# Where the next slot's halves are compared, when q and k are split, and when the ends are turned, in a top-k attention kernel with a feed-forward layer

## The chip, the cores and the metric

The kernel runs on one core of one Trainium2 chip. The metric is the device time of one execution in microseconds (us). Engines are named as in the profile: PE (TensorE; PEld is its weight load), DVE (VectorE), ACT (ScalarE), POOL (GpSimd) and SP (SyncE, which here issues nearly all DMAs).

## The reference

```python
# q, k, v: (8, 8, 576, 64), float32; top_k = 32
scores = (1.0 / np.sqrt(D)) * np.matmul(q, k.transpose(0, 1, 3, 2))
kth = np.partition(scores, -top_k, axis=-1)[..., -top_k:-top_k + 1]
scores = np.where(scores >= kth, scores, -1000000000.0)
scores = scores - np.max(scores, axis=-1, keepdims=True)
attn = np.exp(scores)
attn = attn / (np.sum(attn, axis=-1, keepdims=True) + 1e-09)
x = np.matmul(attn, v).transpose(0, 2, 1, 3).reshape(4608, 512)
h = x @ w_in                                  # (512, 2048)
g = h * (1.0 / (1.0 + np.exp(-1.702 * h)))
out = g @ w_out                               # (2048, 512)
```

Each row of 576 scores keeps its 32 largest; the rest vanish in the softmax. The result goes, head beside head, through a feed-forward layer with a quick GELU.

## The kernel before

**Slots.** The attention is cut into 144 slots, 18 for each batch. A slot is 128 query rows of two heads: four row tiles by four pairs of heads, and two slots that gather the 64 rows left at the end of each head (the "ends"). The first 13 slots (0 to 12, function `slot`) also load and round the weights; from slot 13 on, `two_slots(n)` with odd n lays out two slots at a time. The order of instructions is written out by hand: each engine works off its own queue in the order in which the Python code issues to it, and waits for other engines only through data.

**One slot's way.** `scores` (PE, L295) multiplies q by k into two PSUM tiles. `copy_scores` (ACT, L307) copies them scaled to `sc`. The search (`find`, `topk_of_pairs`, DVE) finds the 32nd largest: `pair_up` compares the halves of each row (L336) into `greater`, and POOL computes the smaller ones without loss in integers, first `sc` less `greater` (L339), then plus the other half (L349) into `lesser`. DVE takes the 32 largest of `greater` by four rounds of MAX8 (L366) with MATCH_REPLACE8 (L369) between them, the 16 largest of `lesser` by two rounds, merges both (L373) and takes the bound, `cut` (L378). `mask` (ACT, L423) and `exps` (ACT, L431, with the sums `den`) follow; `invert` (DVE, L439 and L441) makes the reciprocal `rden`; `normalize` (POOL, L454, two instructions) multiplies. `split` (ACT, L490) parts the words in 16-bit halves over `sc`, SP writes them to DRAM (L492) and reads them back transposed (L498). `values_at` (PE, L557) multiplies by v, and `x_of` (ACT, L571 or L574) copies the result into a row block.

**The feed-forward layer.** Whenever a row block is ready, `hidden` (PE, L618) does a piece of the first layer, for two row blocks together or for one; `tanh` (ACT, L640 and L643) and `gate` (POOL, L652 and L653) make the GELU, and `project` (PE, L673) adds a piece of the second. A finished block leaves through ACT (L681) and SP (L683). One `hidden` and one `project` stand in each slot from slot 13 on, where there is work for them.

**q and k.** They are needed with the head's 64 elements across partitions. `load_both` fetches them (L184, L187) at the slots that `FETCH` gives, counted from a batch's first slot, one entry for each pair of heads. For batch 1, `prepare_by_pe` turns them on PE: `prepare_main` (L217, copied by ACT at L218) and then `prepare_ends` (L222, copied at L223 and L225), which `two_slots` calls through the list `second_part`. From batch 2 on `prepare_by_dma` does it at the slots of `READY`: ACT splits the words into halves (L246), SP writes them to DRAM (L250, L254, L255) and reads them back transposed (L259).

**Within a search.** `find(m)` runs 23 operations: 14 on `greater` (numbers 0 to 13), `pair_up(m + 1)` (14), six on `lesser` (15 to 20), the merge (21) and the bound (22). After number 20 in odd slots and 18 in even ones it calls `invert(m - 1)`. In `two_slots(n)`, POOL's queue gets L339 in the search, then `normalize(n - 1)`, and then `measure(n)`: the lower bounds `lows` (L399), the add of `pair_rest` (L349) and the gate.

Of the kernel before, what the change touches and what calls it, by code (L numbers as in the profile page):

```python
# [9 lines left out]
ALU = mybir.AluOpType  # L10
ENG = mybir.EngineType
F32 = mybir.dt.float32
U32 = mybir.dt.uint32
I32 = mybir.dt.int32
# [4 lines left out]
P = 128  # L19
# [11 lines left out]
def kernel(  # L31
# [27 lines left out]
    nc = tc.nc  # L59

    B, H, S, D = q.shape
# [6 lines left out]
    HALF = S // 2  # L68
# [23 lines left out]
    raws = pool("raws", 7)  # L92
# [24 lines left out]
    raw = {}  # L117
# [154 lines left out]
    second_part = []  # L272
# [8 lines left out]
    N = len(slots)  # L281
    PER = N // B
    st = [{} for _ in slots]
# [45 lines left out]
    greater, lesser = {}, {}  # L329

    def pair_up(n):

        sc = st[n]["sc"]
        a, b = sc[:, :, 0:HALF], sc[:, :, HALF:S]
        greater[n] = lefts.tile([P, 2, HALF], F32, name="greater", tag="left")
        nc.vector.tensor_tensor(out=greater[n][:], in0=a, in1=b, op=ALU.max)  # L336
        lesser[n] = raws.tile([P, 2, HALF], F32, name="lesser", tag="raw")
        whole = lesser[n][:].bitcast(I32)
        nc.gpsimd.tensor_tensor(out=whole, in0=a.bitcast(I32), in1=greater[n][:].bitcast(I32), op=ALU.subtract)  # L339
        unpaired.append(n)  # L340

    unpaired = []
# [1 line left out]
    def pair_rest():  # L344

        while unpaired:
            n = unpaired.pop()
            whole, b = lesser[n][:].bitcast(I32), st[n]["sc"][:, :, HALF:S]
            nc.gpsimd.tensor_tensor(out=whole, in0=whole, in1=b.bitcast(I32), op=ALU.add)  # L349

    def topk_of_pairs(n):

        top = st[n]["top"] = small.tile([P, 2, 2 * TOPK], F32, name="top2", tag="top")
        cut = st[n]["cut"] = small.tile([P, 2], F32, name="cut")
        first, few = greater.pop(n), lesser.pop(n)
        left = lefts.tile([P, 2, HALF], F32, name="left2", tag="left")

        def found(r, i, written=False):
            if r < TOPK // 8:
                at = (8 * r + TOPK) % (TOPK + TOPK // 2)  # L360
                return top[:, i, at : at + 8]
            end = 2 * TOPK - 8 * (r - TOPK // 8) - TOPK
            return top[:, i, end - 1 : end - 9 : -1] if written else top[:, i, end - 8 : end]

        def largest(src, r, i):
            nc.vector.max(found(r, i, True), src[:, i, :])  # L366

        def remove(to, src, r, i):
            nc.vector.match_replace(to[:, i, :], found(r, i), src[:, i, :], LOWEST)  # L369

        def merge():
            both = top[:, :, 0:TOPK].rearrange("p i (s k) -> p i k s", s=2)
            nc.vector.tensor_reduce(  # L373
                out=top[:, :, TOPK + TOPK // 2 :], in_=both, axis=mybir.AxisListType.X, op=ALU.max
            )

        def bound():
            nc.vector.tensor_reduce(  # L378
                out=cut[:], in_=top[:, :, TOPK + TOPK // 2 - 1 :], axis=mybir.AxisListType.X, op=ALU.min, negate=True
            )  # L380

        ops = []
        for r in range(TOPK // 8):
            ops += [lambda r=r, i=i: largest(left if r else first, r, i) for i in range(2)]
            if r < TOPK // 8 - 1:
                ops += [lambda r=r, i=i: remove(left, left if r else first, r, i) for i in range(2)]
        ops += [lambda: pair_up(n + 1) if n + 1 < N else None]
        for r in range(TOPK // 8, TOPK * 3 // 16):
            ops += [lambda r=r, i=i: largest(few, r, i) for i in range(2)]
            if r == TOPK // 8:  # L390
                ops += [lambda r=r, i=i: remove(few, few, r, i) for i in range(2)]
        return ops + [merge, bound]

    def lows(n):

# [40 lines left out]
    def invert(n):  # L436

        some = small.tile([P, 2], F32, name="some", tag="sums")
        nc.vector.tensor_scalar_add(some[:], st[n]["den"][:], 1e-9)  # L439
        rden = st[n]["rden"] = small.tile([P, 2], F32, name="rden", tag="inverse")  # L440
        nc.vector.reciprocal(rden[:], some[:])  # L441
# [44 lines left out]
    def split(n):  # L486

        pr, sc = st[n]["pr"], st[n]["sc"]
        halves = sc[:].rearrange("p i k -> p (i k)").bitcast(U16).rearrange("p (h k) -> p h k", h=2)
        nc.scalar.copy(out=halves, in_=pr[:].bitcast(U16).rearrange("p (k h) -> p h k", h=2))  # L490
        rows = st[n]["rows"] = apart.tile([P, 2, 2 * S], U16, name="rows")
        nc.sync.dma_start(rows[:], halves)  # L492
# [209 lines left out]
    def at(n, fn, *args):  # L702
        later.setdefault(n, []).append((fn, args))
# [1 line left out]

    READY = (-13, -11, -5, -3)
    READY_1 = (-5, -3, -1, 1)
    FETCH = (-17, -15, -9, -7)  # L710
    FETCH_1 = (-11, -9, -4, -2)
    VALUES = (0, 1, 2, 3)
    by_slot = dict(enumerate([2, 2, 3, 3, 3, 3, 3, 3, 3, 3, 2, 2]))
# [12 lines left out]
    for b in range(1, B):  # L726
        for hp in range(NP):
            at(b * PER + (FETCH if b > 1 else FETCH_1)[hp], load_both, b, hp)
            if b > 1:
                at(b * PER + READY[hp], prepare_by_dma, b, hp)  # L730
            else:
# [6 lines left out]
    def finish_one():  # L738
        unfinished.pop(0)()

    def may_project(waiting):

        return len(to_project) > waiting and len(finished) >= NG * CC + to_project[0][1][-1] + 1
# [62 lines left out]
    def bring_all():  # L806

        waiting = len(ready)
        while put_off:
            put_off.pop(0)()  # L810
        if len(ready) > waiting:
            hidden()
# [90 lines left out]
    def two_slots(n):  # L903

        preparing = prepare_by_dma, prepare_by_pe
        todo = [later.pop(m, []) for m in (n, n + 1)]
        live = lambda m: 0 <= m < N
        aside = n < N
        opens = n == SETTLED + 1
        ahead = n < SETTLED + 4  # L910
        assert not any(fn in preparing for fn, _ in todo[1])

        def begin(some):
            for fn, args in some:
                if fn not in preparing:
                    fn(*args)

        def prepare_some():
            for fn, args in todo[0]:
                if fn in preparing:  # L920
                    fn(*args)

        def find(m):
            for i, op in enumerate(topk_of_pairs(m) if live(m) else [lambda: None] * 23):
                op()
                if i == (20 if m % 2 else 18) and live(m - 1):
                    invert(m - 1)
                if i > 1 and unfinished:
                    finish_one()

        def measure(m):
            if live(m):
                lows(m)
            pair_rest()
            gate(aside)

        def project_one():
            if may_project(0):
                project(True)

        if opens:
            bounds(n - 1)
            gate(aside)
        if ahead:
            scores(n + 2)
        if opens:
            bring_all()
        if live(n - 1):
            exponentials(n - 1)
        if ahead:  # L950
            copy_scores(n + 2)
        if opens:
            leave_all()
            tanh(aside)
        prepare_some()
        hidden(ps_t if opens else None)
        while second_part:
            second_part.pop()()
        project_one()
        find(n)  # L960
        if live(n - 1):
            normalize(n - 1)
        tanh(aside)
        measure(n)
        if live(n - 1):
            split(n - 1)
        begin(todo[0])
        if live(n):
            mask(n)
        held = [m for m in (n - 3, n - 2) if live(m) and "rows" in st[m]]  # L970
        if live(n + 2) and not ahead:
            scores(n + 2)
            copy_scores(n + 2)
        o = ps_t.tile([P, 2, P], F32, name="o", tag="tp") if held else None
        for i, m in enumerate(held):
            values_at(m, o[:, i, :])
        if live(n - 1):
            turn_by_dma(n - 1)
        while turns:
            turns.pop(0)()  # L980
        if live(n + 3):
            scores(n + 3)
        if live(n):
            exps(n)
        if held:
            x_of(held, o)
        leave_all()
        hidden(ps_t)
        if live(n + 3):
            copy_scores(n + 3)  # L990
        find(n + 1)
        if live(n):
            normalize(n)
            split(n)
        begin(todo[1])
        if live(n):
            turn_by_dma(n)
        tanh(aside)
        measure(n + 1)
        project_one()  # L1000
        leave_all()
# [39 lines left out]
```

## Time and profile before

| | |
|---|---|
| median of 3 runs | 1469.41 us (1468.19 to 1469.87) |
| the profiled execution's own time | 1469.86 us |
| its span | 1468.0 us |
| busy: PE, PEld, DVE, ACT, POOL | 97%, 69%, 91%, 79%, 66% |
| mean granted clock of TensorE | 0.987 |
| DMA queues, share of 16 engines' span | 62.8% (the main one) |

The profile is one execution. Its span runs from the first instruction to the last; the execution's own time is 1.9 us longer. A busy share is an average over stages: the first 240 us, in which weights are rounded and batch 1 is prepared, the long middle to about 1390 us, in which pairs of slots repeat, and the end, in which the last row blocks go through the feed-forward layer. In the profile each matmul of the source is two instructions. Rows of a group give its source line, engine, operation, output and input tiles, shapes and count; a wait gives the engine and tile that waited, what released it, total us, times and the longest.

### The profile page before, as it was taken

To read this page: it belongs to the slowest core of one execution; us is meant where nothing else is said; L and a number is where in the kernel's file an instruction comes from. 1 tells how busy PE (TensorE), PEld (TensorE's weight loads), DVE (VectorE), ACT (ScalarE), POOL (GpSimd) and SP (SyncE) were. 2 spreads that over 40 slices of the span, in tenths; PEclk is the share of its full clock that TensorE was granted. 3 is DMA by queue.
4 is the path that set the end of the run, shared out by engine and by line. 5 is a ranking of instruction groups with operands and counts; after the bars stand their busy time and mean duration, and the time that the engine had idled before them with its cause. 6 is when DMAs were issued, how large, how long until landed. Compare 5 with 4: busy or idle time off the path is not lost. (4 is left out here: it accounts for less than half of the span.)

```text
span 1468.0 us, 29154 instructions
## 1 busy us (share of the span) xinstructions
PE 1428.0 (97%) x9564; PEld 1006.4 (69%) x9564; DVE 1337.2 (91%) x4672; ACT 1154.8 (79%) x1865; POOL 970.8 (66%) x1171
## 2 busy tenths in 40 slices
PE   7789989999999999999999999999999999999998
PEld 5667746777666667777666667777666667777665
DVE  7999999999999999999999999999999999999910
ACT  6998787878788887878888787888878787778730
POOL 3777666676676776666767667667677666677610
PEclk8899999999999999999999999999999999999999
DMA  7452266767677676776678676776768776644530
GB/s 220 142 156 73 64 169 172 203 170 190 160 196 191 181 176 181 199 183 171 173 189 191 180 180 169 203 185 173 186 175 189 179 192 169 165 131 130 136 88 15
DMA packets 516312, 242.04 MB, mean 165 GB/s; under 512 B 452672, under 2 KB 490560, under 8 KB 516160
## 3 DMA queue, kind: packets, MB, share of 16 engines
q1 hardware_dynamic: 515728, 239.89, 62.8%
q8 instruction: 75, 1.23, 0.4%
q14 instruction: 77, 0.63, 0.1%
q10 hardware_dynamic: 432, 0.30, 0.1%
HBM read 45.09 MB, written 102.24 MB: 100 GB/s over the span
## 5 line engine op out<-in xcount | busy, mean ns | idle before, releaser
L618 PEld LDWEIGHTS ph<-xT,win 128*128 128x128 f32 x3520 | 484.7, 191 | 89.0 <-issue 52.6
L618 PE MATMUL ph<-xT,win 128*128 128x128 f32 (+1 forms) x3520 | 538.0, 309 | 3.8 <-ACT xT L574 2.9
L673 PE MATMUL po<-wout,th 128*128 128x512 f32 x1152 | 522.3, 596 | 0.0
L490 ACT COPY sc<-pr 128x2304 uint16<-128x2304 uint16 x132 | 279.0, 2113 | 153.8 <-POOL pr L454 153.7
L673 PEld LDWEIGHTS po<-wout,th 128*128 128x128 f32 x1152 | 214.8, 192 | 214.5 <-issue 209.0
L366 DVE MAX8 top<-left 128x8 f32<-128x288 f32 x792 | 320.9, 446 | 0.0
L339 POOL TENSOR_TENSOR lesser<-sc,greater 128x576 int32<-128x576 int32 x132 | 186.3, 1411 | 195.2 <-DVE greater L336 194.5
L454 POOL TENSOR_SCALAR pr<-pr,rden 128x576 f32<-128x576 f32 x264 | 194.1, 748 | 125.8 <-DVE top L373 85.9
L369 DVE MATCH_REPLACE8 left<-top,left 128x288 f32<-128x288 f32 x528 | 229.6, 442 | 0.0
L431 ACT ACTIVATE pr<-sc,low 128x576 f32<-128x576 f32 x288 | 219.6, 767 | 0.0
L366 DVE MAX8 top<-lesser 128x8 f32<-128x288 f32 x528 | 213.7, 446 | 0.0
L423 ACT ACTIVATE sc<-sc,cut 128x576 f32<-128x576 f32 x288 | 207.4, 770 | 6.5 <-POOL cut L410 3.8
L295 PE MATMUL s_ps<-qk_t 64*128 64x288 f32 (+1 forms) x1280 | 190.3, 433 | 0.2 <-ACT qk_t L218 0.2
L349 POOL TENSOR_TENSOR lesser<-lesser,sc 128x576 int32<-128x576 int32 x132 | 186.5, 1413 | 0.2
L307 ACT ACTIVATE sc<-s_ps 128x576 f32<-128x576 f32 x288 | 170.3, 644 | 4.8 <-PE s_ps L295 3.4
L653 POOL TENSOR_TENSOR th<-th,h 128x512 f32<-128x512 f32 x129 | 165.3, 1282 | 10.8
L295 PEld LDWEIGHTS s_ps<-qk_t 64*128 64x128 f32 (+1 forms) x1280 | 106.2, 178 | 80.1 <-issue 57.8
L640 ACT ACTIVATE th<-ph 128x512 f32<-128x512 f32 x144 | 85.5, 594 | 76.0 <-PE ph L618 72.1
L557 PE MATMUL o<-pt,v_l 128*64 128x128 f32 (+1 forms) x2368 | 143.5, 264 | 0.0
L557 PEld LDWEIGHTS o<-pt,v_l 128*64 128x64 f32 x2368 | 119.8, 137 | 26.9 <-issue 18.4
L336 DVE TENSOR_TENSOR greater<-sc 128x576 f32<-128x576 f32 x132 | 99.8, 756 | 40.0 <-ACT sc L307 40.0
L652 POOL TENSOR_SCALAR th<-th 128x512 f32<-128x512 f32 x129 | 80.0, 620 | 57.7 <-ACT th L640 57.7
(78 smaller groups left out, 1386.6 us busy)
## 6 DMA issues: line engine op xcount, KB each, us to landing
rows<-sc SPq DMA_DIRECT2D x132, 576.0 KB, 3.2
qk_rows<-halves SPq DMA_DIRECT2D x48, 256.0 KB, 2.8
qk_l<-in_q_dram SPq DMA_DIRECT2D x64, 128.0 KB, 3.3
raw<-in_moe_w_in_dram SPq DMA_DIRECT2D x16, 512.0 KB, 4.6
v_l<-in_v_dram SPq DMA_DIRECT2D x32, 256.0 KB, 3.7
raw<-in_moe_w_out_dram SPq DMA_DIRECT2D x16, 512.0 KB, 3.5
out_dram<-ob SPq DMA_DIRECT2D x32, 256.0 KB, 2.9
qk_l<-in_k_dram SPq DMA_DIRECT2D x62, 128.0 KB, 3.0
```

What stands on the lines that cost most here:

```text
L295: nc.tensor.matmul(ps[i][rows, c, 0:HALF], lhsT=qT[b, hps[p]][on, cols], rhs=kT[b, hps[p]][on, FIRST[i] + c * HALF : FIRST[i] + (c + 1) * ...
L339: nc.gpsimd.tensor_tensor(out=whole, in0=a.bitcast(I32), in1=greater[n][:].bitcast(I32), op=ALU.subtract)
L349: nc.gpsimd.tensor_tensor(out=whole, in0=whole, in1=b.bitcast(I32), op=ALU.add)
L366: nc.vector.max(found(r, i, True), src[:, i, :])
L369: nc.vector.match_replace(to[:, i, :], found(r, i), src[:, i, :], LOWEST)
L423: nc.scalar.activation(sc[:, i, :], sc[:, i, :], AF.Prelu, bias=cut[:, i : i + 1], alpha=HUGE)
L431: nc.scalar.activation(pr[:, i * S : (i + 1) * S], sc[:, i, :], AF.Exp, bias=low[:, i : i + 1], accum_out=den[:, i : i + 1],)
L454: nc.gpsimd.tensor_scalar(pr[:, i, :], pr[:, i, :], st[n]["rden"][:, i : i + 1], 1.0, op0=ALU.mult, op1=ALU.mult)
L490: nc.scalar.copy(out=halves, in_=pr[:].bitcast(U16).rearrange("p (k h) -> p h k", h=2))
L557: nc.tensor.matmul(o[j * D : (j + 1) * D, cols], lhsT=main[:, j, c, :] if c < NF else tail[:, j, :], rhs=pt[:, MAIN[j] + c if c < NF else ...
L618: nc.tensor.matmul(ph[:, i * many * P : (i + 1) * many * P], lhsT=win[:, c, f * P : (f + 1) * P], rhs=xs[:, first : first + step * (many - ...
L673: nc.tensor.matmul(x.po[:], lhsT=gT[:, i * P : (i + 1) * P], rhs=wout[:, f, :], start=(x.done == 0), stop=(x.done == FC - 1))
```

## The change

Three things move.

- The next slot's halves are compared after the bound of a search, as its last operation, and no longer between the rounds on `greater` and those on `lesser`. POOL's subtract moves from there into `pair_rest`, directly ahead of the add. The numbers of the operations on `lesser` fall by one, and the reciprocal of the sums is called after number 17 in odd slots (after the removals from `lesser`) and 19 in even ones (after its second maxima).
- The slots at which q and k are split for batches 2 to 7 change from -13, -11, -5, -3 to -13, -9, -5, -1, counted from the batch's first slot, and the third fetch from -9 to -11.
- The ends of batch 1's q and k (slots 13, 15, 17 and 19) are turned behind the projection, the search's issue and the split of the slot before, and no longer ahead of the projection.

```diff
@@ pair_up
         nc.vector.tensor_tensor(out=greater[n][:], in0=a, in1=b, op=ALU.max)
-        lesser[n] = raws.tile([P, 2, HALF], F32, name="lesser", tag="raw")
-        whole = lesser[n][:].bitcast(I32)
-        nc.gpsimd.tensor_tensor(out=whole, in0=a.bitcast(I32), in1=greater[n][:].bitcast(I32), op=ALU.subtract)
         unpaired.append(n)
@@ pair_rest
             n = unpaired.pop()
-            whole, b = lesser[n][:].bitcast(I32), st[n]["sc"][:, :, HALF:S]
+            a, b = st[n]["sc"][:, :, 0:HALF], st[n]["sc"][:, :, HALF:S]
+            lesser[n] = raws.tile([P, 2, HALF], F32, name="lesser", tag="raw")
+            whole = lesser[n][:].bitcast(I32)
+            nc.gpsimd.tensor_tensor(out=whole, in0=a.bitcast(I32), in1=greater[n][:].bitcast(I32), op=ALU.subtract)
             nc.gpsimd.tensor_tensor(out=whole, in0=whole, in1=b.bitcast(I32), op=ALU.add)
@@ topk_of_pairs
-        ops += [lambda: pair_up(n + 1) if n + 1 < N else None]
         for r in range(TOPK // 8, TOPK * 3 // 16):
...
-        return ops + [merge, bound]
+        return ops + [merge, bound, lambda: pair_up(n + 1) if n + 1 < N else None]
@@ the schedule
-    READY = (-13, -11, -5, -3)
+    READY = (-13, -9, -5, -1)
...
-    FETCH = (-17, -15, -9, -7)
+    FETCH = (-17, -15, -11, -7)
@@ find
-                if i == (20 if m % 2 else 18) and live(m - 1):
+                if i == (17 if m % 2 else 19) and live(m - 1):
                     invert(m - 1)
@@ two_slots
         hidden(ps_t if opens else None)
-        while second_part:
-            second_part.pop()()
         project_one()
         find(n)
...
             split(n - 1)
+        while second_part:
+            second_part.pop()()
         begin(todo[0])
```

## The prediction

> **What bounds the kernel now.** I read the page first, then the busy time by stage, the waits, and the timelines of PE, ACT, DVE and POOL over one repeat of the work. The page's busy lines say that PE is full and DVE close behind:
>
> ```profile
> PE 1428.0 (97%) x9564; PEld 1006.4 (69%) x9564; DVE 1337.2 (91%) x4672; ACT 1154.8 (79%) x1865; POOL 970.8 (66%) x1171
> ```
>
> By stage, in a stretch of the middle (columns: stretch, length, busy PE, PEld, DVE, ACT, POOL, clock, DMA share, GB/s):
>
> ```profile
> 440.00:640.00 200.00, 200.00 (x1296) 140.24 (x1295) 191.29 (x698) 163.90 (x253) 139.42 (x169) 1.00 0.72 186
> ```
>
> PE never pauses there, and DVE idles 8.7 us of 200. A busy PE can still be a stretched one, so I took the time from the first scores of one pair of slots to those of the next, in PE's timeline. Quiet pairs take 18.65 us while the first layer's matmuls serve two row blocks (719.71 to 738.36), 18.89 while they serve one (586.16 to 605.05), and inside them each matmul follows the last at its shortest spacing (0.215 us for 256 columns). DVE, read from one cut (L378) to the same a pair later, has its own rate: 18.79 us in quiet pairs of either sort. Two loops of almost the same length run side by side, and two sorts of stall sit on top. The waits name the first:
>
> ```profile
> DVE greater L336 <- ACT sc L307: 40.0, 63, 1.3
> ```
>
> Once in a pair DVE stands still, 0.5 us in quiet pairs, because the next slot's scores are not yet copied. With the overlap of successive instructions that is lost there (0.08) it is 0.6, so DVE's own work is about 18.2 us a pair; the pair 185.96 to 204.12, in which it never waits, took 18.16. The second stall shows in ACT's timeline:
>
> ```profile
> 617.03 0.60 ACT L681 ACTIVATE ob<-po 128x512 f32<-128x512 f32 x1 [1.40 <-PE po L673]
> ...
> 620.37 2.10 ACT L246 COPY halves<-qk_l 128x2304 uint16<-128x2304 uint16 x1
> ...
> 623.33 2.12 ACT L490 COPY sc<-pr 128x2304 uint16<-128x2304 uint16 x1
> ...
> 626.69 1.18 ACT L307 ACTIVATE sc<-s_ps 128x576 f32<-128x576 f32 x2
> ```
>
> An output block leaves (L681, behind a wait of 1.40 for PE), and a preparation of q and k (L246, 2.1 us) follows in the same pair. ACT is late for L307, and the scores that need those PSUM tiles are stretched on PE from 1.24 to 1.72:
>
> ```profile
> 608.54 1.24 PE L295 MATMUL s_ps<-qk_t 64*128 64x288 f32 x8
> ...
> 627.43 1.72 PE L295 MATMUL s_ps<-qk_t 64*128 64x288 f32 x8
> ```
>
> **What the Trainium skill says.** "Perfetto Trace Analysis", Identifying the Most-Contended Engine, holds that matmul busy time does not tell how full TensorE is; here 100% busy goes with both 18.65 and 19.73 us a pair, hence the spacings above. The same page, Optimization Strategy, says that a gap repeated on the engine that should be full can mean too little PSUM: so here, the two score tiles not being emptied in time. "SBUF — State Buffer", Who interferes with whom, says that a DVE instruction with two SBUF inputs and a GpSimd instruction that reads SBUF exclude each other, whole instructions long, the first to start winning. The trace has it once:
>
> ```profile
> 153.11 1.29 POOL L144 TENSOR_TENSOR wout<-wout,raw 128x512 int32<-128x512 int32 x1
> 153.28 1.73 DVE L336 TENSOR_TENSOR greater<-sc 128x576 f32<-128x576 f32 x1
> 154.47 1.69 POOL L147 TENSOR_TENSOR wout<-wout,raw 128x512 f32<-128x512 f32 x1
> ```
>
> The comparison, 0.74 us elsewhere, ended 0.61 after POOL's instruction; POOL's next, 1.29 elsewhere, took 1.69. All other 131 comparisons now start while POOL is idle or in its last 0.1 us.
>
> **The change, part by part.** No instruction is added or removed; their order moves.
>
> (1) The spacing. Preparations move in each batch from slots -13, -11, -5, -3 to -13, -9, -5, -1. In the trace L681 falls in slots 25, 29, 33, 39, 43, 47, 51, 55, 57, 61, 65, 69 and so on. Every second preparation of two (25, 33, 43, 51, 61, 69) meets one, no first one does (23, 31, 41, 49, 59, 67), and the new places (27, 35, 45, 53, 63, 71) are free of it. Stalled pairs on PE, less the quiet 18.65 or 18.89 (and 0.17 where an end slot's values take 2.49 instead of 2.32): 0.48, 0.91, 0.59, 0.43, that is 2.4 us in each 36 slots, three times over batches 2 to 7: 7.2 us. A lone preparation (599.59) costs PE nothing and I cost the new places at nothing; what hides it is ACT's wait for POOL (0.84 there) ahead of L490. Loads move with it: six DMA issues at -11 instead of -9. They hold SP some 5 us (589.47 to 594.15 at another slot) ahead of a transpose of probabilities; the values that need it start at 606, after its landing at about 599. The buffer it fills is free since -13. The last k and q (slot -1) land some 5 us after issue, 7 us ahead of their scores. Cost 0.
>
> (2) The comparison at the end of the search. The scores are there 3 us earlier than needed, so the 0.6 us goes. Late next would be the inverse of the sums (L439), which waits for exps (L431): in slots with an L681 these end (620.47) just as the inverse is reached today, so DVE will wait there up to 1.5 us in every second pair. PE does not feel it while DVE has slack. On POOL the subtract (1.41) now stands behind the two multiplies and lows, directly ahead of the add; POOL's idle time ahead of it (194.5 us in all) covers it. The add is done some 5.7 us after the reciprocal at worst, and its result is read at some 7.5 (the comparison and 14 operations later); the gate behind it feeds a projection 3.2 us after its end (712.98 to 716.18) and starts at most 1.4 later. Cost 0.
>
> But the comparison now falls beside POOL's multiplies, which start 0.33 after the reciprocal and read SBUF:
>
> ```profile
> 716.33 0.17 DVE L441 RECIPROCAL rden<-some 128x2 f32<-128x2 f32 x1
> 716.42 0.20 DVE L373 TENSOR_REDUCE top<-top 128x32 f32<-128x64 f32 x1
> 716.65 0.19 DVE L378 TENSOR_REDUCE cut<-top 128x2 f32<-128x34 f32 x1
> 716.66 0.75 POOL L454 TENSOR_SCALAR pr<-pr,rden 128x576 f32<-128x576 f32 x1 [1.25 <-DVE top L373]
> 716.75 0.81 DVE L366 MAX8 top<-greater 128x8 f32<-128x288 f32 x2
> ```
>
> With R for the reciprocal's start, POOL multiplies from R+0.33 to 1.07 and 1.07 to 1.80. In odd slots a pair of MAX8 comes between, and the comparison starts at R+1.28, inside the second: by the instance above it ends at 1.80+0.61 = 2.41 instead of 2.02, 0.4 late. In even slots it starts where the last line shows, R+0.42, 0.09 after POOL. If POOL holds the port it ends at 1.07+0.61 = 1.68 instead of 1.16, 0.5 late; if DVE does, POOL loses 0.6, which is hidden. POOL's start is not its first read: L147 above was held until 0.54 after its start and lost 0.39, so it needs the port about 0.15 in, and a multiply by a pointer sets up longer (0.27 for one element at L399, 0.19 for two at L411). I take DVE as first, by little. So DVE needs 18.2+0.4 = 18.6, or 19.1.
>
> (3) The ends behind the projection, four times (slots 13 to 19). PE's waits there (3.2 and 3.9 longest) vanish, but two of the four lie where PE has no first-layer work and DVE sets the pace. ACT's copies of the ends now follow a projection of 3.6 us, which can delay mask by 0.8 in slots 13 and 15. Between -1.6 (DVE's waits up to there: 1.08 and 0.52) and +1; I take 0.
>
> **Sum.** With DVE at 18.6, PE sets the pace: 7.2 from (1), and 0.4 in each 36 slots (over slots 20 to 142, 1.4) that PE now loses to DVE's 18.79 when it runs at 18.65, of which I take half. 1469.86 - 7.9 = 1462.0 against the profiled execution's own time; the median of the runs lies 0.45 lower, so 1461.5.
>
> **The rivals.** A, the case above: 48%, 1457 to 1467. B, slower: POOL is first to the port in even slots as well. Then DVE needs 18.2+0.4+0.5 = 19.1 and is the bound; from 166.62 to 1396.54 there are 65 pairs of 18.92, so 65 x 0.19 = 12 us more: 1481.5, or 1477 to 1490 if POOL's delay of 0.6 comes on top through L490. It decides from 0.3 us a comparison. For it: POOL starts first on paper and the one instance; against it: the set-up. 41%. C, nearly nothing: the race goes both ways by turns, POOL first in some two even slots of three; DVE then averages 18.9, what it averages now, and what (1) gives PE is lost: 1467 to 1472, 8%. D: PE holds at 18.65 and 18.89 but ACT is late at the new places too, so that (1) moves the stalls instead of removing them: 1468, 3%, half of it in "faster".
>
> **Numbers.** Predicted 1461.5. A measurement of this kernel tells about 0.2%, 2.9 us, from no change. A gives faster but for a small tail (47), D adds 2: faster 0.49, same 0.09, slower 0.42. The range must hold both signs: 1457 to 1487; A's own is 1457 to 1467.
>
> **What would show it.** Right: PE's pairs at 18.65 and 18.89 everywhere, scores at 1.24 beside each L246, no wait at L336, one at L439 instead, comparisons near 0.74 in even slots and 1.15 in odd ones. Wrong: comparisons of 1.1 or more in all slots, DVE without waits at 19 us a pair, and PE with gaps.

## The result, and the profile after

The changed kernel takes 1493.21 us (median of 4 runs, 1491.95 to 1493.7), the kernel before 1469.62 beside it: a ratio of 1.0161 [1.0144, 1.0179] (in brackets the 95% interval), slower by 24 us. Of the runs below, one execution of the kernel with the comparison alone came at a lower granted clock (0.93, against 0.985 to 0.991 in all others) and took 1514.43 us; it is left out of that kernel's time. The profiled execution's own time is 1493.47, its span 1491.5. In it the lines below 336 stand one lower: L337 and up are subtract and add (L348, L349), merge L373 and `cut` L378 as before, mask L422, exps L430, sums L438, reciprocal L440, multiplies L453, split L489, `hidden` L617, `project` L672, the block that leaves L680.

The page's busy lines:

```profile
PE 1446.2 (97%) x9564; PEld 1012.8 (68%) x9564; DVE 1371.1 (92%) x4672; ACT 1148.2 (77%) x1865; POOL 1041.7 (70%) x1171
```

The stretch of the middle, with the columns of before:

```profile
440.00:640.00 200.00, 198.38 (x1300) 137.21 (x1298) 193.57 (x686) 160.42 (x252) 147.37 (x164) 1.00 0.71 181
```

The count of instructions is the same, and POOL is busy for 71 us more (970.8 before): its instructions became longer, by 40 us the multiplies (234.1 after 194.1) and by 0.5 one of the two `lows` in each odd slot (0.77 after 0.27). PE, which never paused in this stretch, now does. DVE still idles 6.4 us of 200, so it isn't simply full. Its waits say for what; POOL and ACT have theirs beside it (waits of the changed kernel: engine, tile, line, released by; total us, times, longest):

```profile
ACT sc L489 <- POOL pr L453: 249.7, 105, 4.7
...
DVE some L438 <- ACT pr L430: 31.1, 35, 6.1
```

The wait at L336 (40.0 us) is gone, as predicted, and one at the sums for exps stands in its place, as predicted. The first line has grown: ACT's wait to split until POOL has multiplied was shorter before:

```profile
ACT sc L490 <- POOL pr L454: 153.7, 117, 3.4
```

The time, read from one `cut` (L378) on DVE to the same a pair of slots later: before, 65 pairs took 1229.9 us; after, 1254.8 (165.20 to 1420.02). The first four of them (slots 14 to 21) took 20.80, 18.80, 18.81 and 22.18 instead of 19.34, 18.16, 18.80 and 19.37: 4.9 us, where the ends are turned. The other 61 took 20.0 more. They alternate: 19.00 without a block that leaves in the pair, 19.49 with one; before, such a block by itself made hardly any difference (18.79 in most pairs of either sort). The timeline of one pair of the changed kernel, lines of DVE, POOL and ACT (here and below, "odd" and "even" name the slot in whose search a comparison or a reciprocal stands; the reciprocal itself is that of the slot before):

```profile
505.07 0.17 DVE L440 RECIPROCAL rden<-some 128x2 f32<-128x2 f32 x1
...
505.41 2.09 POOL L453 TENSOR_SCALAR pr<-pr,rden 128x576 f32<-128x576 f32 x2 [3.12 <-DVE top L373]
505.49 0.75 DVE L336 TENSOR_TENSOR greater<-sc 128x576 f32<-128x576 f32 x1
...
507.53 2.11 ACT L489 COPY sc<-pr 128x2304 uint16<-128x2304 uint16 x1 [3.61 <-POOL pr L453]
...
510.50 1.45 ACT L422 ACTIVATE sc<-sc,cut 128x576 f32<-128x576 f32 x2
...
512.61 0.77 ACT L430 ACTIVATE pr<-sc,low 128x576 f32<-128x576 f32 x1
...
512.94 0.44 DVE L369 MATCH_REPLACE8 lesser<-top,lesser 128x288 f32<-128x288 f32 x1
513.27 0.19 ACT L430 ACTIVATION_READ_ACCUMULATOR pr<-sc,low 128x1 f32 x1
...
513.50 0.17 DVE L438 TENSOR_SCALAR some<-den 128x2 f32<-128x2 f32 x1
513.70 0.17 DVE L440 RECIPROCAL rden<-some 128x2 f32<-128x2 f32 x1
...
514.04 1.47 POOL L453 TENSOR_SCALAR pr<-pr,rden 128x576 f32<-128x576 f32 x2 [1.25 <-DVE rden L440]
...
514.98 1.14 DVE L336 TENSOR_TENSOR greater<-sc 128x576 f32<-128x576 f32 x1
...
524.09 0.17 DVE L440 RECIPROCAL rden<-some 128x2 f32<-128x2 f32 x1
```

The reader is to see two things. **The port.** In the even slot (505.49) the comparison takes its 0.75 and POOL's two multiplies 2.09 instead of 1.47: DVE came second by 0.08 and was served first. In the odd slot (514.98) it starts inside the second multiply, takes 1.14, and holds up POOL's `lows` in turn. Both are what the prediction took. **The loop.** From the even slot's reciprocal (505.07) POOL's held multiplies lead to the split, that to mask (behind two instructions of ACT for the GELU), mask to exps, and exps to the odd slot's sums at 513.50: 8.63 us from reciprocal to reciprocal. ACT waits 3.61 for POOL ahead of the split, so each delay of POOL goes through in full. From the odd reciprocal (513.70) DVE's own work leads to the next even one (524.09): 10.39. Together 19.02, the pair. DVE itself could have issued the odd sums 0.20 earlier (the last MATCH_REPLACE8 at 512.94 and its usual spacing of 0.36), so its own work is 18.80; where a block leaves, ACT's 0.6 lies on the same chain, and the pair is 19.49.

Before, the same way had slack. DVE went from an even reciprocal (706.46) to the next odd one (716.33) in 9.87, and exps were done at 714.24, 1.91 ahead of the odd sums:

```profile
706.46 0.17 DVE L441 RECIPROCAL rden<-some 128x2 f32<-128x2 f32 x1
...
708.30 2.11 ACT L490 COPY sc<-pr 128x2304 uint16<-128x2304 uint16 x1 [1.52 <-POOL pr L454]
...
714.04 0.20 ACT L431 ACTIVATION_READ_ACCUMULATOR pr<-sc,low 128x1 f32 x1
...
716.15 0.15 DVE L439 TENSOR_SCALAR some<-den 128x2 f32<-128x2 f32 x1
```

### The profile page after: what moved, and what is told of

Its sections match the earlier page's. It is cut to its first block, busy times and chain, and to the rows that moved or that the text cites. A ratio compares the mean times of both kernels' runs of the same rounds, so it can differ in the third digit from the quotient of the medians.

```text
span 1491.5 us, 29016 instructions
## 1 busy us (share of the span) xinstructions
PE 1446.2 (97%) x9564; PEld 1012.8 (68%) x9564; DVE 1371.1 (92%) x4672; ACT 1148.2 (77%) x1865; POOL 1041.7 (70%) x1171
## 5 line engine op out<-in xcount | busy, mean ns | idle before, releaser
L617 PEld LDWEIGHTS ph<-xT,win 128*128 128x128 f32 x3520 | 486.3, 191 | 89.5 <-issue 54.4
L617 PE MATMUL ph<-xT,win 128*128 128x128 f32 (+1 forms) x3520 | 541.0, 310 | 2.8 <-ACT xT L573 1.9
L672 PE MATMUL po<-wout,th 128*128 128x512 f32 x1152 | 521.5, 596 | 1.9 <-ACT ob L680 1.9
L489 ACT COPY sc<-pr 128x2304 uint16<-128x2304 uint16 x132 | 279.2, 2115 | 249.7 <-POOL pr L453 249.7
L453 POOL TENSOR_SCALAR pr<-pr,rden 128x576 f32<-128x576 f32 x264 | 234.1, 899 | 316.6 <-DVE top L373 203.3
L672 PEld LDWEIGHTS po<-wout,th 128*128 128x128 f32 x1152 | 212.7, 191 | 218.7 <-issue 208.0
L430 ACT ACTIVATE pr<-sc,low 128x576 f32<-128x576 f32 x288 | 220.1, 771 | 2.4 <-POOL low L398 2.4
L422 ACT ACTIVATE sc<-sc,cut 128x576 f32<-128x576 f32 x288 | 207.9, 774 | 6.2 <-POOL cut L409 5.3
L295 PE MATMUL s_ps<-qk_t 64*128 64x288 f32 (+1 forms) x1280 | 201.1, 434 | 8.6 <-ACT sc L307 4.5
L349 POOL TENSOR_TENSOR lesser<-lesser,sc 128x576 int32<-128x576 int32 x132 | 186.9, 1416 | 10.4
L348 POOL TENSOR_TENSOR lesser<-sc,greater 128x576 int32<-128x576 int32 x132 | 186.1, 1410 | 1.2 <-DVE greater L336 1.2
L295 PEld LDWEIGHTS s_ps<-qk_t 64*128 64x128 f32 (+1 forms) x1280 | 110.4, 178 | 95.1 <-issue 35.3
L336 DVE TENSOR_TENSOR greater<-sc 128x576 f32<-128x576 f32 x132 | 123.4, 935 | 0.0
L369 DVE MATCH_REPLACE8 lesser<-top,lesser 128x288 f32<-128x288 f32 x264 | 114.9, 443 | 0.0
L369 DVE MATCH_REPLACE8 left<-top,greater 128x288 f32<-128x288 f32 x264 | 114.9, 443 | 0.0
```

The source lines that it names most:

```text
L295: nc.tensor.matmul(ps[i][rows, c, 0:HALF], lhsT=qT[b, hps[p]][on, cols], rhs=kT[b, hps[p]][on, FIRST[i] + c * HALF : FIRST[i] + (c + 1) * ...
L422: nc.scalar.activation(sc[:, i, :], sc[:, i, :], AF.Prelu, bias=cut[:, i : i + 1], alpha=HUGE)
L430: nc.scalar.activation(pr[:, i * S : (i + 1) * S], sc[:, i, :], AF.Exp, bias=low[:, i : i + 1], accum_out=den[:, i : i + 1],)
L453: nc.gpsimd.tensor_scalar(pr[:, i, :], pr[:, i, :], st[n]["rden"][:, i : i + 1], 1.0, op0=ALU.mult, op1=ALU.mult)
L617: nc.tensor.matmul(ph[:, i * many * P : (i + 1) * many * P], lhsT=win[:, c, f * P : (f + 1) * P], rhs=xs[:, first : first + step * (many - ...
L672: nc.tensor.matmul(x.po[:], lhsT=gT[:, i * P : (i + 1) * P], rhs=wout[:, f, :], start=(x.done == 0), stop=(x.done == FC - 1))
```

## Experiments

Times are ratios to the kernel before on the same chip. Edits are against the changed kernel unless said otherwise; lengths of pairs come from L378 as above.

**One part at a time: the comparison.** The kernel before with the comparison last, the subtract beside the add, and the reciprocal after 17 and 19; spacing and ends as before.

> The kernel before with the comparison moved to the end of the search (and the inverse after operation 17 or 19), q and k and the ends as before. Theory L (a loop: the comparison stands beside POOL's multiplies; in even slots POOL's first multiply is held 0.6 us, and the delay goes through split, mask and exps to the odd slot's inverse, which DVE now reaches sooner and waits for): pairs at 19.0 us, 19.5 with a block's eviction in them, total 1486 to 1494, ratio 1.011 to 1.017. Rival T (the new places of q and k and their transfers cost the time): total within 4 us of before.

1487.16 us, 1.0123 [1.0103, 1.0144]. Pairs of 19.0 and 19.5, multiplies of 897 ns in the mean, as in the full change. This part alone costs 18.6 us by the medians (1468.54 before), with q and k at their old places: the loop is its doing. Of the 4.9 us in the first four pairs, 2.6 are here too, without the ends moved.

**One part at a time: the spacing.** The kernel before with

```diff
-    READY = (-13, -11, -5, -3)
+    READY = (-13, -9, -5, -1)
-    FETCH = (-17, -15, -9, -7)
+    FETCH = (-17, -15, -11, -7)
```

> The kernel before with only READY and FETCH changed. Theory L: the pairs in which an eviction met a preparation lose their extra 0.4 to 0.9 us, nothing else moves: 1460 to 1466, ratio 0.993 to 0.998. Rival T: 1475 or more. Scores (L295) beside L246 at 1.24 by L, stretched by T.

1462.08 us, 0.9952 [0.9937, 0.9967]. The pairs of 19.6 are gone: behind the first five, all but the last (18.13) lie between 18.78 and 18.96. The wait ahead of the comparison shows it (waits of this kernel; the longest was 1.3 before):

```profile
DVE greater L336 <- ACT sc L307: 32.3, 63, 0.5
```

The 7.2 us of step (1) measure 6.5. In the changed kernel they are not seen, because there the loop sets the pace: 18.6 of the comparison and 4.4 of the ends make 23.0 of the 23.6 without it.

**One part at a time: the ends.** The kernel before with the ends behind projection and split in all four slots.

> The kernel before with only the ends turned behind the projection. The trace of the changed kernel shows the pair of slots 20 and 21 at 22.2 us (19.4 before) and slots 14 and 15 at 20.8 (19.3 before), with scores waiting 3.5 us for the copy of the ends: theory E, the ends cost 2 to 5 us: 1472 to 1475. Rival: those pairs are long because of the comparison, and the ends alone give within 1 us of before or a gain.

1472.93 us, 1.0028 [1.0017, 1.0039]: +4.4 by the medians. The pair after slot 13 takes 19.80 (19.34 before), after 17 19.13 (18.80), after 19 21.71 (19.37).

**Which of the ends.** The same, in slot 19 alone:

> The kernel before, with the ends behind the projection in slot 19 alone. In the run with all four moved, the pair that follows slot 19 took 21.71 us instead of 19.37, the pair after slot 13 19.80 instead of 19.34, that after slot 17 19.13 instead of 18.80. Theory (slot 19 is the costly one, because only there do the scores of slot 21 wait on PE for ACT's copy of the ends): +2 to +3 us, 1471.6 to 1472.6, the pair after slot 19 at 21.5 or more and the others as before. Rival (every slot costs about the same, and the long pair only collects what the three before it have put off): about +1.1 us, 1470.7, that pair below 20.5.

1472.49 us, 1.0021 [1.0012, 1.0031], +3.3 by the medians; the pair after slot 19 takes 21.84, all others are as before. And in slots 13, 15 and 17 alone:

> The kernel before, with the ends behind the projection in slots 13, 15 and 17 and not in 19. Theory (slot 19 is the costly one): +0.5 to +1.5 us, 1470.1 to 1471.1, the pair after slot 19 within 0.3 us of the 19.37 before. Rival (every slot costs the same, or the delay is handed on): +3 us or more, 1472.6 or more, and that pair above 20.5.

1469.31 us, 0.9999 [0.9991, 1.0008]; the pair after 19 takes 18.79. So the cost is slot 19's. The first three add nothing that shows, less than the 0.5 to 1.5 expected: what they lose (0.46 and 0.33) is mostly made good in the pair after slot 19. The timeline with the ends late in slot 19 alone shows how:

```profile
225.24 2.11 ACT L490 COPY sc<-pr 128x2304 uint16<-128x2304 uint16 x1 [3.96 <-POOL pr L454]
227.26 0.21 ACT L223 COPY qk_t<-tp 128x64 f32<-128x64 f32 x1
227.36 0.33 ACT L225 COPY qk_t<-tp 128x64 f32<-128x64 f32 x2
...
227.63 2.29 PE L295 MATMUL s_ps<-qk_t 64*128 64x288 f32 x6 [5.55 <-ACT qk_t L225]
```

The copies of the ends stand on ACT behind the split, and the split waits 3.96 for POOL. The scores of that slot read those ends, and PE, which works in order, stands still 5.55 us; its matmuls behind the pause then take longer, these scores 2.29 for six instructions instead of 1.24 for eight and the values that follow 1.97 instead of 1.09. In the kernel before, the same copies were done at 221.0, PE had a projection to do until 226.30, and scores and values ran at 1.24 and 1.09.

**The port alone.** The reciprocal after 19 in both slots:

```diff
-                if i == (17 if m % 2 else 19) and live(m - 1):
+                if i == 19 and live(m - 1):
```

> The changed kernel with the inverse after operation 19 in odd slots too (17 there now). Theory L: DVE reaches the inverse 0.8 us later in odd slots, so it stops waiting for exps, and the odd comparison comes ahead of POOL's read too, so it falls from 1.13 to 0.75 us; DVE's own work is then 18.4 us a pair and PE sets the pace: 1460 to 1470. Rival P (what matters is the port: each multiply that is held costs its 0.6 us wherever it stands): POOL is held in both slots, so no better than 1490.

1472.61 us, 1.0022 [1.0012, 1.0032]: one number gives back 20.6 of the 24 us, though not all that was expected (1460 to 1470). And yet POOL is held in both slots now, not in one of two (the page's groups: instruction count, then total us, mean ns of one, idle time before):

```profile
L453 POOL TENSOR_SCALAR pr<-pr,rden 128x576 f32<-128x576 f32 x264 | 271.4, 1039 | 289.8 <-DVE top L373 276.9
```

899 ns in the mean in the changed kernel, 748 before. In some slots DVE is held as well. Of the 130 comparisons beside a multiply, 106 start 0.064 to 0.091 us behind it and take 0.75; the other 24 start 0.095 to 0.101 behind it and take 1.25, since there POOL's first multiply is served first and the comparison holds only its second. One of the 24:

```profile
623.57 1.96 POOL L453 TENSOR_SCALAR pr<-pr,rden 128x576 f32<-128x576 f32 x2 [3.26 <-DVE top L373]
623.66 1.25 DVE L336 TENSOR_TENSOR greater<-sc 128x576 f32<-128x576 f32 x1
```

A pair of slots needs at least 18.29 on DVE (18.79 with one such comparison), and from one reciprocal to the next 9.15 in either half, more than the 8.63 of the chain. So the hold by itself doesn't set the pace; the hold with an early odd reciprocal does. It isn't free either: with the ends' 4 us taken off, this kernel stands near the kernel before and not the spacing's 6.5 below it. How these 6 us divide between the hold, the 24 lost comparisons and DVE's waits for exps in pairs with a leaving block was not tested.

The reciprocal after 17 in both slots:

> The changed kernel with the inverse after operation 17 in even slots too (19 there now). The even comparison then falls inside POOL's second multiply, as the odd one does, so DVE is held 0.4 us in both slots and POOL's first multiply in neither. Theory L: the chain behind the even inverse is 0.6 shorter, the wait for exps goes, and DVE's own work (18.2 + 0.23 + 0.76) sets 19.1 to 19.2 us in every pair, with an eviction in it or not: 1483 to 1491. Rival (POOL's loss costs nothing, the odd slot's early inverse alone makes the wait): pairs still differ by 0.5 with an eviction, total as the changed kernel or slower.

1497.57 us, 1.0196 [1.0181, 1.0211]. All comparisons fall into a multiply, and POOL is held nowhere:

```profile
L336 DVE TENSOR_TENSOR greater<-sc 128x576 f32<-128x576 f32 x132 | 147.9, 1120 | 0.0
...
L453 POOL TENSOR_SCALAR pr<-pr,rden 128x576 f32<-128x576 f32 x264 | 193.3, 745 | 330.9 <-DVE rden L440 307.5
```

Pairs take 19.31 with a leaving block or without, and DVE waits for exps 12.8 us in all instead of 31.1: here DVE's own work is the bound. A shorter pair and 1483 to 1491 had been expected; the sum below shows what was missing.

**Loop or hold.** The comparison of even slots ahead of the reciprocal, of odd slots as changed:

```diff
-        return ops + [merge, bound, lambda: pair_up(n + 1) if n + 1 < N else None]
+        compare = lambda: pair_up(n + 1) if n + 1 < N else None
+        return ops + ([merge, bound, compare] if n % 2 else [compare, merge, bound])
-                if i == (17 if m % 2 else 19) and live(m - 1):
+                if i == (17 if m % 2 else 20) and live(m - 1):
```

> The changed kernel with the comparison of even slots ahead of the reciprocal (now after number 20), and of odd slots as changed. POOL's multiplies are then no longer held in even slots. Theory (a loop through both slots: from the reciprocal of an even slot over POOL's two multiplies, the split, mask and exps to the reciprocal of the odd slot, 8.63 us, and from there DVE's own work to the next even reciprocal, 10.39 us): the first part falls by the 0.62 of the hold to 8.01, the second grows by the comparison of 0.75 to 11.14, so pairs take 19.15, and 19.6 where an output block leaves: 3 to 10 us above the changed kernel, 1496 to 1503. Rival (the hold of POOL is the whole cost, 0.6 a pair): pairs at 18.4 on DVE, PE the bound again, 20 us below the changed kernel, about 1472.

1492.20 us, 1.0160 [1.0146, 1.0174]. The hold of POOL is gone, and nothing is won:

```profile
504.83 0.17 DVE L441 RECIPROCAL rden<-some 128x2 f32<-128x2 f32 x1
505.16 1.47 POOL L454 TENSOR_SCALAR pr<-pr,rden 128x576 f32<-128x576 f32 x2 [3.79 <-DVE top L373]
...
512.63 0.17 DVE L439 TENSOR_SCALAR some<-den 128x2 f32<-128x2 f32 x1 [0.29 <-ACT pr L431]
512.84 0.17 DVE L441 RECIPROCAL rden<-some 128x2 f32<-128x2 f32 x1
...
523.89 0.17 DVE L441 RECIPROCAL rden<-some 128x2 f32<-128x2 f32 x1
```

The chain takes 8.01 (504.83 to 512.84), as expected, and DVE's part 11.05 (11.14 expected): pairs of 19.06, and 19.55 with a leaving block. What POOL no longer loses, the comparison adds to the other half of the loop. The 65 pairs take 2.4 us more than in the changed kernel. The total is below what was expected all the same, since the first of them begins 1.0 us sooner and what comes behind the last is 1.8 shorter, neither of which the expectation had.

**The comparison off the port and off the loop.** Ahead of merge and bound in both slots, with the reciprocal behind it:

```diff
-        return ops + [merge, bound, lambda: pair_up(n + 1) if n + 1 < N else None]
+        return ops + [lambda: pair_up(n + 1) if n + 1 < N else None, merge, bound]
-                if i == (17 if m % 2 else 19) and live(m - 1):
+                if i == 20 and live(m - 1):
```

> The changed kernel with the comparison one step up: behind the last maxima of lesser and ahead of the inverse, in both slots; merge and bound follow. POOL is then idle while DVE compares. Theory L (the loop, closed by the clash at the port and by the early inverse): comparisons at 0.75 us, multiplies at 0.75 us each, DVE's own work 18.2 us a pair and no loop, so PE sets the pace: about 1462 plus the 4.4 us of the ends, 1462 to 1469. Rival R (the subtract and the add standing together in POOL's queue, not the port, make POOL late): no better than 1480.

1463.02 us, 0.9958 [0.9943, 0.9972]: subtract and add still stand together in POOL's queue, so that is not what makes POOL late. The same with the ends back ahead of the projection, which is the spacing of the change and a better place for its comparison:

> As the kernel with the comparison ahead of the inverse, and the ends of batch 1 turned ahead of the projection as before; the spacing of q and k stays. Theory L: 1457 to 1463, at or a little below the 1462 of the spacing alone, since DVE no longer waits at the comparison and PE is the bound. Rival R: 1476 or more.

1458.79 us, 0.9930 [0.9915, 0.9944]: faster than both kernels by 10 and 34 us. Its stretch of the middle and two of its waits:

```profile
440.00:640.00 200.00, 200.00 (x1330) 138.98 (x1330) 190.61 (x702) 167.57 (x257) 140.24 (x171) 1.00 0.72 187
```

```profile
ACT sc L489 <- POOL pr L453: 94.2, 89, 2.7
...
DVE some L438 <- ACT pr L430: 53.3, 35, 6.9
```

Multiplies take 745 ns in the mean, comparisons 756 in the median. DVE does a pair in 18.03 where it isn't held, and waits for exps longer than in the changed kernel, 53.3 us. That wait is now slack, since PE is full: the same row, on the path there and off it here.

**Two inputs or one.** The comparison as a reduction over the two halves, which reads one SBUF operand:

```diff
-        nc.vector.tensor_tensor(out=greater[n][:], in0=a, in1=b, op=ALU.max)
+        nc.vector.tensor_reduce(
+            out=greater[n][:], in_=sc[:].rearrange("p i (s k) -> p i k s", s=2), axis=mybir.AxisListType.X, op=ALU.max)
```

> The changed kernel with the comparison done as a reduction over two strided halves, which reads one SBUF tensor of 1152 elements a row instead of two of 576. If two inputs are what clashes with POOL: multiplies back at 0.75 us each beside the reduction, which takes 1.2 to 1.4 us in all slots alike; DVE's own work rises to some 19.5 us a pair, total 1500 to 1520. If the neighbourhood in the queue is to blame and not the port: multiplies held as now, and reductions of two lengths.

1520.45 us in a single execution. The groups of its page (lines one lower again):

```profile
L452 POOL TENSOR_SCALAR pr<-pr,rden 128x576 f32<-128x576 f32 x264 | 193.9, 747 | 383.1 <-DVE top L372 218.9
...
L335 DVE TENSOR_REDUCE greater<-sc 128x576 f32<-128x1152 f32 x132 | 180.7, 1369 | 0.0
```

All 132 reductions take 1361 to 1381 ns, in even slots and odd, and no multiply is held. It is too slow to be of use, but it rules out the neighbourhood in the queue: reductions start beside the multiplies as the comparisons did, and hold none. That fits the second SBUF input as what clashes with POOL; as the operation is another one too, this run alone does not prove it.

**One sum for DVE.** From these runs DVE's own work in a pair can be put together. It is 18.03 with each comparison clear of POOL and another instruction between it and the first MAX8 that reads it. MAX8 straight behind the comparison that wrote its input adds 0.13 a slot: 18.29 with it in both, as the reciprocal after 19 shows. A merge straight behind the last MAX8, with no reciprocal between, adds 0.12 (0.48 from one to the other instead of 0.36). A comparison inside a multiply adds 0.38, a reduction 0.62.

| | sum | measured |
|---|---|---|
| before: one merge behind MAX8 | 18.03 + 0.12 = 18.15 | 18.16 |
| changed: both MAX8, one merge, one clash | 18.03 + 0.26 + 0.12 + 0.38 = 18.79 | 18.80, and 19.00, 19.49 on the loop |
| reciprocal after 17: both, two merges, two clashes | 18.03 + 0.26 + 0.24 + 0.76 = 19.29 | 19.31 |
| even comparison first: one MAX8, one merge, one clash | 18.03 + 0.13 + 0.12 + 0.38 = 18.66 | 18.69, and 19.06, 19.55 on the loop |
| reductions: both, one merge, two reductions | 18.03 + 0.26 + 0.12 + 1.24 = 19.65 | 19.67 |

The 18.03 comes from the kernels with the comparison ahead of merge and bound, the 0.13 from the one with the reciprocal after 19; the others are differences of single steps in the traces. The five rows test their sum.

## Why the prediction was wrong

It gave 1461.5, from 1457 to 1487, with faster as the likeliest; the kernel is at 1493.2, beyond even rival B's 1490.

- **The base** was read rightly: DVE's 18.16 of own work, PE's pairs of 18.65 and 18.89, two loops of almost one length.
- **Step (1), the spacing.** Right by itself: 7.2 predicted, 6.5 measured. In the changed kernel the pace is DVE's, and nothing of it is left.
- **The race at the port.** Right in what came of it: DVE is first in even slots, and the comparison takes 0.75; in odd slots 1.14 for the 1.15 predicted. The margin was luck. The prediction had POOL need the port 0.15 us or more behind its start; the kernel with the reciprocal after 19 puts the turn between 0.091 and 0.095, and in the changed kernel the comparison comes 0.083 to 0.088 behind POOL in all even slots but one (0.059). By these figures rival C's race, which goes both ways, was less than 0.01 us away. "SBUF — State Buffer", Who interferes with whom, in the Trainium skill holds that two SBUF inputs clash with a GpSimd instruction that reads SBUF, that one input does not, and that the first to issue blocks the other for its whole instruction. The traces agree (multiplies of 1364 ns, comparisons of 1.13 us, reductions untouched), with one difference: by the recorded starts POOL is first by 0.08 us and still the one that waits.
- **"If DVE does, POOL loses 0.6, which is hidden".** This is the step that failed. In even slots ACT waits for POOL ahead of the split (3.61 us in the pair shown), so nothing on the way hides it: it goes through split, mask and exps into the odd reciprocal, and the chain takes 8.63 instead of 8.01. The prediction gives no reason for "hidden". It names ACT's wait for POOL ahead of L490 itself, in step (1) as what hides a preparation and under rival B as a way for the 0.6 to count, and the row (153.7 us) stood in the waits of before; its own sum leaves the wait out.
- **"PE does not feel it while DVE has slack".** The wait at the sums was foreseen, even to its place, and then treated as a cost beside the loop. It closes a loop. Before, DVE's part from the even reciprocal to the odd one was 9.87, and the slack of 1.9 took up a leaving block (there exps end at 620.47, just as DVE comes to the sums). The change then moved the odd reciprocal ahead of the second maxima of `lesser` and the even one behind them (two MAX8, 0.72, each time), which cut DVE's part from 9.87 to 8.43, and the held multiplies made the chain 8.63. Both were needed: without the hold the chain would be the shorter one (8.01, where it was seen without it), and with the reciprocal after 19 the hold stays and the loop is gone. The prediction moved the two reciprocals with the rest and gave them no step of their own. The slack was missing on the other side too: own work of 18.6 was 18.80.
- **The sum for DVE** lacked 0.26 and took the merge as it was: that an instruction straight behind the one that wrote its input starts later was in no term.
- **Step (3), the ends.** "I take 0" measured +4.4. The delay was sought at mask in slots 13 and 15; it came in slot 19, where the copies fall behind a split that waits for POOL, and PE waits for them. The bound of +1 was too tight since it came from what the copies delay, and not from what delays the copies.
- **Rival B** had nearly the right size of DVE's pair (19.1, for 19.00 and 19.49) by chance: POOL wasn't first. "Wrong: comparisons of 1.1 or more in all slots" fits the kernel with the reciprocal after 17, not the change.

The parts add up within their intervals: 18.6 for the comparison and 4.4 for the ends are 23.0, against 23.6 measured, with the spacing worth nothing while DVE is behind.

## What to carry to other kernels

When a profile shows an engine waiting for another at every repeat, a delay of the second is not hidden by the second's idle time: follow the chain from it until it returns to the engine where it began, and compare its length with that engine's own work between the two points. An operation that is moved along a queue changes that work on both sides of every point that others wait for, here the reciprocal, so each such point needs its own sum. Before copies that others need are moved behind another instruction, look at what that one waits for: here it was a split that waits for POOL.

## What the runs showed of the hardware

- DVE can win the port although POOL's record starts earlier. In the changed kernel, the comparison alone and the reciprocal after 19, all 234 comparisons that start up to 0.091 us behind the start of one of POOL's multiplies are served first (0.75 us). All that start 0.095 to 0.235 behind one, in these and in the kernels with the reciprocal after 17 and the even comparison first, wait for it and take 1.11 to 1.26. So a few ns of the recorded starts decide who waits. Which of the two engines' records lies off from its first read can't be told from these runs.
- MAX8 that reads a tile which the instruction just ahead of it wrote starts 0.11 to 0.13 us later than one that reads another tile, and a reduction behind the MAX8 that wrote its input 0.12 later. "VectorE: DVE Perf Modes", The DRAIN you can't avoid, says that the next operation doesn't start until the pipe is empty, and that one which isn't held starts earlier; here MAX8 of 0.45 follow each other in 0.36, and the extra appears only with the dependence.
- One number in a schedule, where the reciprocal of the sums stands, moved the time by 20.6 us without a change in any engine's list of work.
